# Attention and two gated layers on one core: the first batch's value products, one float32 product or split float32r products

## The chip, the cores and the metric

The kernel runs on one core of a Trainium2 chip. Its time is the device time of one execution in microseconds (us). The engines are PE (matrix products; PEld is its weight load), ACT (activations), DVE (vector), POOL and SP, which here only issues DMAs. Each engine takes its instructions in a fixed order and waits at one whose inputs are not there.

## The reference

Three steps follow each other: block-causal attention, a gated layer, and a gated layer behind a root-mean-square norm.

```
scores = scale * q @ k^T                 # 4 batches, 8 heads, 576 tokens, head width 64
mask   = row // 64 >= column // 64       # causal by blocks of 64 tokens
attn   = exp(scores - max) / (sum + 1e-9)
x      = attn @ v                        # then (2304, 512): all heads side by side
x      = ((x @ w_a) * (x @ w_b)) @ w_out # 512 -> 1536 -> 512
xn     = x / rms(x) * rms_g
out    = (silu(xn @ w_gate) * (xn @ w_val)) @ w_out2
```

Everything is float32 in and out.

## The kernel before

**Two ways to multiply.** A float32 product is one matmul in the program and two records of PE in the trace. A split product writes each operand as hi + lo, both of the type float32r (hi is a float32r copy, lo the remainder), and adds up the products of the parts; each of those is one record. The gated layers use split products throughout (`wh xh + wh xl + wl xh`, L598 to L600).

**Attention** goes by pairs of heads, 16 in all (4 batches, 4 pairs each); pair m has key tiles of 128 rows (index j) and 9 blocks of 64 queries (index b, L326: one buffer `pp8`, `pp7`, ... per b, shared by all pairs). A pair is done in two parts, blocks 0 to 5 and blocks 6 to 8. The generator `attention` (L306) lets three pairs' parts run abreast: in unit u it issues the value products of part u-2, the scores of part u, and the transposes of part u-1. For one part the chain is:

- `score` (L384): product of keys and queries on PE (L392, tiles `s` and `mm`), row maximum on DVE (L395, L398, L399), exponential on ACT with the row sum as a by-product (L401). After certain blocks DVE forms the reciprocals (L409, L410, tile `rt`) and POOL scales each block's probabilities with them (L413, tile `pp`).
- `p_transposes` (L416): PE transposes 128 x 128 squares, four to a PSUM bank (L428, tile `t`, three banks), and ACT copies a bank to SBUF (L431). For batches from WHOLE on the copy is hi (`ph`), and DVE writes lo (`pl`, L434) from the same bank. For batches below WHOLE the copy is plain float32 (`pw`), and there is no lo.
- The values. `whole_values` (L437), for batches below WHOLE: one float32 product per key tile for both heads at once (L453); of the result ACT copies one head and DVE the other to `xf` (L462, recorded at the copy helper's L109 and L111), in groups of four blocks at most. `values` (L469), for the others: per head one matmul with hi and one with lo of the probabilities (L488), against a tile `vv` that holds v's hi and lo side by side, so that both come out in one go in different partitions; ACT copies one half to `xf` (L493) and DVE adds the other (L494).
- `vv` is made by `make_vv` (L375) on POOL: a copy (L112) and a subtraction (L382). It is issued in unit u = 2m, two units ahead of its use; it returns at once where v was loaded whole.

v comes in by `load_v` (L353), two DMAs of SP per pair: below WHOLE with the heads interleaved in the tile (runs of 64 numbers), otherwise in runs of 5 x 64 numbers.

**Order of the work.** Batch 0's attention runs first (L885), with the first nine weight pieces made every ninth step of it (`prepare`, L189: loads by SP, decoding on ACT, DVE and POOL at L144 to L149, splitting at L109 and L119). Of the first gated layer only 27 matmuls can run beside it: three PSUM banks, three of the four column groups of x that are already there, three matmuls each. From there on the first gated layer's blocks run with batches 1 to 3 of attention between their matmuls, and the second gated layer at the end. Each engine's order is chosen by a scheduler that works out its own timeline when the program is built; so a changed instruction count moves neighbours too.

Of the kernel before, what the change touches and what calls it, by code (L numbers as in the profile page):

```python
# [25 lines left out]

BACKGROUND = (0, 4, 8, 24)

WHOLE = 1

RING = 19
UNSCALE = 2.0 ** -8
# [17 lines left out]
def tile_attention_moe_moe(  # L50
# [255 lines left out]
    def attention(pools, x_of, done):  # L306
# [46 lines left out]
        def load_v(m):  # L353
            b, h = divmod(m, H // 2)
            if b < WHOLE:
                t = vv[m] = ap2.tile([P, NTILE, 2, D], F32, tag="vr", name="vr", bufs=3)
# [59 lines left out]
        def p_transposes(u):  # L416
            m, part = divmod(u, 2)
            places = PLACE[part]
            whole = m // (H // 2) < WHOLE
            if whole:  # L420
# [90 lines left out]
        for u in range(2 * NP + 2):  # L511
            m, part = divmod(u, 2)
            if u >= 2:
                yield from (whole_values if (u - 2) // H < WHOLE else values)(u - 2)
            sc = list(SCORED[part]) if m < NP else []
# [592 lines left out]
```

## Time and profile before

| | |
|---|---|
| time, median of 3 runs | 1063.22 us (1061.3 to 1063.79) |
| the profiled execution's own time | 1065.04 us |
| its span in the trace | 1063.3 us |
| busiest engines, share of the span | PE 99%, DVE 63%, ACT 57%, POOL 37% |

Busy shares are averages over the whole span. The attention of batch 0 takes the first 77 us, and there PE is busy nine tenths of the time rather than all of it; the 80 us and more that follow show PE busy without a gap. A record of PE lasts longer than the time until the next record can begin, since matmuls overlap; so the cost of a run of matmuls is read from the start of the first to the start of what follows.

### The profile page before, as it was taken

Reading aid. Unit: us, or ns where it says so; the run is one execution under the profiler, and the core shown is the slowest. Engines: PE = TensorE matmul, PEld = TensorE weight load, DVE = VectorE, ACT = ScalarE, POOL = GpSimd, SP = SyncE. Lnnn points to the kernel's source line nnn. Section 1 sums busy time; section 2 is a strip of 40 time slices with the busy share of each in tenths; the row PEclk is TensorE's granted clock in tenths of the full one; section 3 lists DMA queues with packets and bytes.
Section 4 is the critical chain, followed back from the end, with each engine's and each line's share of the span. In section 5 each row is a group of like instructions: output and inputs, shape, how many; then the busy total and the mean of one; then the engine's idle time right before and its main releaser. Section 6 shows DMA issues by size and latency. Waiting matters only on the chain.

```text
span 1063.3 us, 16723 instructions
## 1 busy us (share of the span) xinstructions
PE 1048.8 (99%) x5644; PEld 933.9 (88%) x5644; DVE 669.4 (63%) x1299; ACT 602.1 (57%) x1334; POOL 396.5 (37%) x408
## 2 busy tenths in 40 slices
PE   9989999999999999999999999999999999999998
PEld 6668888889888888888878788999999999999998
DVE  6557778556675575385375724792876929657285
ACT  7878888557665664256444522744656546455352
POOL 5755668234444453175455501120231202212020
PEclk9999999999999999999999999999999999999999
DMA  9776877768986676878879763788889788887883
GB/s 240 223 237 217 283 243 279 283 226 275 310 309 209 218 250 239 315 260 315 343 277 358 271 257 134 225 281 255 251 280 326 259 273 250 290 270 229 275 249 116
DMA packets 121371, 276.52 MB, mean 260 GB/s; under 512 B 35779, under 2 KB 48835, under 8 KB 110790
## 3 DMA queue, kind: packets, MB, share of 16 engines
q1 hardware_dynamic: 121286, 275.46, 76.9%
q8 instruction: 45, 0.74, 0.3%
q14 instruction: 40, 0.33, 0.1%
HBM read 214.05 MB, written 61.36 MB: 259 GB/s over the span
## 4 chain that ended last, share of the span: by engine, by line
PE 77%; POOL 4%; issue 4%; DMA 4%; ACT 3%; DVE 2%; SPq 0%; POOLq 0%; ACTq 0%; DVEq 0%
PE mm L626 25%; PE mm L657 12%; PE mm L599 6%; PE mm L600 6%; PE mm L598 6%; PE s L392 5%; PE t L488 4%; PE t L428 3%; PE mm L558 3%; PE mm L560 3%; PE mm L559 3%; POOL src L149 2%; POOL bg L240 1%; DMA wc<-bg 1%; DMA st<-in_w_ab_dram 1%
## 5 line engine op out<-in xcount | busy, mean ns | idle before, releaser
L598 PE MATMUL mm<-xh,ab 128*128 128x512 f32 (+1 forms) x480 | 183.0, 384 | 0.0
L599 PE MATMUL mm<-xl,ab 128*128 128x512 f32 (+1 forms) x480 | 182.6, 380 | 0.0
L600 PE MATMUL mm<-xh,ab 128*128 128x512 f32 (+1 forms) x480 | 181.1, 377 | 0.0
L626 PE MATMUL mm<-hT,w 128*128 128x384 f32 x576 | 165.5, 337 | 1.4 <-ACT mm L634 1.4
L119 POOL TENSOR_TENSOR hl<-g,hh 128x384 fp32r<-128x384 f32 x36 | 42.7, 1187 | 299.6 <-ACT hh L109 299.6
L626 PE MATMUL mm<-hB,w 128*128 128x384 f32 x432 | 125.9, 336 | 0.0
L657 PE MATMUL mm<-hh,w 128*128 128x384 f32 x504 | 125.2, 336 | 0.0
L413 POOL TENSOR_SCALAR pp<-pp,rt 128x64 f32<-128x64 f32 (+3 forms) x144 | 79.9, 569 | 110.6 <-DVE rt L410 46.9
L634 ACT ACTIVATE mm<-mm 128x384 f32<-128x384 f32 x144 | 66.8, 474 | 75.3 <-PE mm L626 42.5
L626 PEld LDWEIGHTS mm<-hT,w 128*128 128x128 f32 x576 | 105.9, 188 | 2.8 <-ACT mm L634 2.5
L599 PEld LDWEIGHTS mm<-xl,ab 128*128 128x128 f32 x480 | 90.9, 189 | 16.7 <-issue 1.0
L600 PEld LDWEIGHTS mm<-xh,ab 128*128 128x128 f32 x480 | 90.9, 189 | 16.3 <-issue 0.7
L598 PEld LDWEIGHTS mm<-xh,ab 128*128 128x128 f32 x480 | 90.5, 189 | 16.3 <-issue 1.1
L626 PE MATMUL mm<-lT,w 128*128 128x384 f32 x288 | 96.9, 337 | 0.0
L392 PE MATMUL s<-ks,qz 128*128 128x64 f32 (+4 forms) x284 | 91.6, 412 | 2.4 <-ACT pp L401 2.3
L401 ACT ACTIVATE pp<-s,st 128x288 f32<-128x288 f32 (+8 forms) x142 | 70.2, 497 | 37.1 <-DVE st L395 28.9
L657 PEld LDWEIGHTS mm<-hh,w 128*128 128x128 f32 x504 | 90.6, 188 | 0.4 <-ACT mm L634 0.4
L657 PE MATMUL mm<-hl,w 128*128 128x384 f32 x252 | 81.4, 336 | 0.0
L626 PEld LDWEIGHTS mm<-hB,w 128*128 128x128 f32 x432 | 79.5, 188 | 0.0
L559 PE MATMUL mm<-hh,o 128*128 128x512 f32 (+1 forms) x208 | 79.3, 382 | 0.0
L558 PE MATMUL mm<-hh,o 128*128 128x512 f32 (+1 forms) x208 | 78.3, 377 | 0.5 <-DVE acc L568 0.5
L560 PE MATMUL mm<-hl,o 128*128 128x512 f32 (+1 forms) x208 | 76.6, 375 | 0.0
(146 smaller groups left out, 2317.4 us busy)
## 6 DMA issues: line engine op xcount, KB each, us to landing
w<-wc SPq DMA_DIRECT2D x252, 256.0 KB, 3.4
ab<-wab SPq DMA_DIRECT2D x36, 1024.0 KB, 5.6
w<-wco SPq DMA_DIRECT2D x126, 256.0 KB, 3.4
wc<-bg SPq DMA_DIRECT2D x12, 1792.0 KB, 6.8
o<-wo SPq DMA_DIRECT2D x12, 1536.0 KB, 7.4
st<-in_w_ab_dram SPq DMA_DIRECT2D x34, 512.0 KB, 4.8
wab<-ab SPq DMA_DIRECT2D x12, 1024.0 KB, 5.2
wco<-bg SPq DMA_DIRECT2D x6, 1792.0 KB, 7.0
```

The costliest lines, as they stand in the source:

```text
L392: pe.matmul(ps[:, 0:z - a], qz[m % 2][:, b], ks[m][:, a:z], start=True, stop=True)
L401: act.activation(pi[:, a:z], pss[x][:, 0:z - a], AF.Exp, bias=s[:, b:b + 1], scale=1.0, accum_out=t3[:, b, x:x + 1],)
L413: pool.tensor_scalar(t, t, r[:, y:y + 1], 1.0, ALU.mult, ALU.mult)
L558: pe.matmul(ps[:, 0:n], wh, hh, start=(y == 0), stop=False)
L559: pe.matmul(ps[:, 0:n], wl, hh, start=False, stop=False)
L560: pe.matmul(ps[:, 0:n], wh, hl, start=False, stop=(y == TF - 1))
L598: pe.matmul(ps[:, 0:n], wh[:, a:z], xhc, start=(c == 0), stop=False)
L599: pe.matmul(ps[:, 0:n], wh[:, a:z], xlc, start=False, stop=False)
L600: pe.matmul(ps[:, 0:n], wl[:, a:z], xhc, start=False, stop=(c == KC - 1))
L626: pe.matmul(ps, lhs, rhs[:, c, :], start=(start and c == 0 and y == 0), stop=(c == 1 and y == 2), skip_group_check=not start,)
L634: act.activation(to, ps, AF.Copy)
L657: pe.matmul(banks[m], lhs, rhs, start=(start and f == group[0] and y == 0), stop=(f == group[-1] and y == 2), skip_group_check=not start,)
```

## The change

```diff
-WHOLE = 1
+WHOLE = 0
```

With WHOLE at 0 no batch is below it. For the four pairs of batch 0, `load_v` takes the second form, `make_vv` does its two POOL operations, `p_transposes` writes `ph` and `pl` instead of `pw`, and `values` takes the place of `whole_values`. `whole_values` (L437 to L467) is not called any more. The code that batch 0 now goes through is that of batches 1 to 3:

```python
            copy(pool, hi, t)                                            # L381
            pool.tensor_tensor(lo, t, hi.bitcast(F32), ALU.subtract)
...
                    dve.tensor_tensor(lo, ps[:, 0:n], hi.bitcast(F32), ALU.subtract)   # L434
...
                act.activation(x[r, h, cols], ps[z, 0:n], AF.Copy)       # L493
                dve.tensor_tensor(x[r, h, cols], ps[r, 0:n], x[r, h, cols], ALU.add)
```

On POOL, at the first pair of heads, before (`pp_158` to `pp_163` are blocks b = 3 to 8, `rt` the reciprocals, `ks` the scaled keys of a later pair):

```order
L413 TENSOR_SCALAR pp_157<-pp_157,rt_139 128x192
L413 TENSOR_SCALAR pp_158<-pp_158,rt_139 128x256
L413 TENSOR_SCALAR pp_159<-pp_159,rt_139 128x320
L413 TENSOR_SCALAR pp_160<-pp_160,rt_139 128x384
L413 TENSOR_SCALAR pp_163<-pp_163,rt_139 128x576
L413 TENSOR_SCALAR pp_161<-pp_161,rt_139 128x448
L413 TENSOR_SCALAR pp_162<-pp_162,rt_139 128x512
L370 TENSOR_SCALAR ks<-kr 128x576
```

and now:

```order
L413 TENSOR_SCALAR pp_157<-pp_157,rt_139 128x192
L413 TENSOR_SCALAR pp_158<-pp_158,rt_139 128x256
L112 TENSOR_SCALAR vv<-vr 128x10x64
L413 TENSOR_SCALAR pp_159<-pp_159,rt_139 128x320
L413 TENSOR_SCALAR pp_160<-pp_160,rt_139 128x384
L112 TENSOR_SCALAR vv<-vr 128x10x64
L382 TENSOR_TENSOR vv<-vr,vv 128x10x64
L413 TENSOR_SCALAR pp_163<-pp_163,rt_139 128x576
L382 TENSOR_TENSOR vv<-vr,vv 128x10x64
L370 TENSOR_SCALAR ks<-kr 128x576
L413 TENSOR_SCALAR pp_161<-pp_161,rt_139 128x448
L413 TENSOR_SCALAR pp_162<-pp_162,rt_139 128x512
```

Two pairs' `vv` (a copy and a subtraction each) now stand between the normalisations of the first pair, and the part-1 blocks `pp_161` and `pp_162` come behind them and behind `ks`.

On DVE, where the second pair's scores and the first pair's transposes meet, before (`st` are row maxima, `x` a weight piece that is being decoded):

```order
L395 TENSOR_REDUCE st_138<-mm 128x1
L409 TENSOR_REDUCE rt_139<-su_141 128x2
L410 RECIPROCAL rt_139<-rt_139 128x2
L395 TENSOR_REDUCE st_138<-mm 128x1
L398 TENSOR_REDUCE st_138<-mm 128x1
L395 TENSOR_REDUCE st_138<-s 128x1 x2
L148 TENSOR_SCALAR x<-a 128x512
```

and now:

```order
L395 TENSOR_REDUCE st_138<-mm 128x1
L434 TENSOR_TENSOR pl_253<-t,ph_252 128x512
L395 TENSOR_REDUCE st_138<-mm 128x1
L409 TENSOR_REDUCE rt_139<-su_141 128x2
L398 TENSOR_REDUCE st_138<-mm 128x1
L410 RECIPROCAL rt_139<-rt_139 128x2
L148 TENSOR_SCALAR x<-a 128x512
L395 TENSOR_REDUCE st_138<-s 128x1
L434 TENSOR_TENSOR pl_253<-t,ph_252 128x512
L395 TENSOR_REDUCE st_138<-s 128x1
L434 TENSOR_TENSOR pl_253<-t,ph_252 128x512
L395 TENSOR_REDUCE st_138<-mm 128x1
```

Three subtractions `pl` have come in among the row maxima that release the exponentials. The second gated layer's order is the same in both.

## Rows read from the trace of the kernel before

**Rows 1.** The page's first part: busy time, share of the span, instructions.

```profile
PE 1048.8 (99%) x5644; PEld 933.9 (88%) x5644; DVE 669.4 (63%) x1299; ACT 602.1 (57%) x1334; POOL 396.5 (37%) x408
```

**Rows 2.** Stretches: us, busy us per engine (instructions), granted clock, DMA share, GB/s.

```profile
6.00:20.00 14.00, 13.98 (x65) 9.80 (x65) 10.94 (x34) 11.63 (x40) 7.51 (x13) 1.00 1.12 253
20.00:45.00 25.00, 21.85 (x107) 15.12 (x105) 14.18 (x43) 22.84 (x65) 18.57 (x25) 1.00 0.95 291
45.00:77.00 32.00, 28.54 (x138) 21.17 (x137) 17.06 (x42) 23.83 (x65) 20.42 (x25) 1.00 0.61 189
6.00:77.00 71.00, 64.37 (x305) 46.09 (x305) 42.18 (x117) 58.29 (x168) 46.50 (x62) 1.00 0.83 237
```

**Rows 3.** PE in time order: start, us, engine, line, operation [idle before].

```profile
17.80 1.03 PE L453 MATMUL t<-pw,vr 128*128 128x256 f32 x4
18.66 0.60 PE L428 MATMUL t<-ident,pp 128*128 128x128 f32 x4
```

**Rows 4.** PE in time order, split value products of batch 1.

```profile
105.54 0.27 PE L488 MATMUL t<-ph,vv 128*128 128x192 f32 x1
...
105.99 0.21 PE L488 MATMUL t<-ph,vv 128*128 128x64 f32 x1
...
106.15 0.55 PE L428 MATMUL t<-ident,pp 128*128 128x128 f32 x3
...
118.88 0.33 PE L488 MATMUL t<-pl,vv 128*128 128x384 f32 x1
119.06 0.28 PE L488 MATMUL t<-ph,vv 128*128 128x256 f32 x1
...
119.29 0.22 PE L488 MATMUL t<-ph,vv 128*128 128x128 f32 x1
119.35 0.38 PE L392 MATMUL s<-ks,qz 128*128 128x64 f32 x2
```

**Rows 5.** By line: instructions, ns min/median/max, first and last start, forms.

```profile
L434 DVE TENSOR_TENSOR pl<-t,ph x84: 278/682/694, 76.7 to 422.6; 128x512 fp32r<-128x512 f32 x72, 128x128 fp32r<-128x128 f32 x12
L494 DVE TENSOR_TENSOR xf<-t,xf x48: 329/449/562, 91.0 to 427.9; 64x384 f32<-64x384 f32 x24, 64x192 f32<-64x192 f32 x24
L493 ACT ACTIVATE xf<-t x48: 322/406/491, 90.5 to 427.0; 64x384 f32<-64x384 f32 x24, 64x192 f32<-64x192 f32 x24
L111 DVE COPY xf<-t x12: 294/360/428, 17.6 to 75.3; 64x256 f32<-64x256 f32 x4, 64x128 f32<-64x128 f32 x4, 64x192 f32<-64x192 f32 x4
L109 ACT ACTIVATE xf<-t x12: 253/314/400, 17.0 to 73.8; 64x256 f32<-64x256 f32 x4, 64x128 f32<-64x128 f32 x4, 64x192 f32<-64x192 f32 x4
L112 POOL TENSOR_SCALAR vv<-vr x12: 720/726/1167, 49.9 to 365.5; 128x640 fp32r<-128x640 f32 x12
L382 POOL TENSOR_TENSOR vv<-vr,vv x12: 1548/1568/2267, 52.9 to 366.4; 128x640 fp32r<-128x640 f32 x12
```

**Rows 6.** POOL in time order, pair 0's normalisation.

```profile
13.79 1.31 POOL L413 TENSOR_SCALAR pp<-pp,rt 128x448 f32<-128x448 f32 x2 [0.62 <-DVE rt L410]
```

**Rows 7.** DVE, POOL and ACT in time order around one stall.

```profile
20.43 0.69 DVE L119 TENSOR_TENSOR ab<-x,ab 128x512 fp32r<-128x512 f32 x1 [0.41 <-ACT ab L109]
...
52.87 2.11 DVE L119 TENSOR_TENSOR ab<-x,ab 128x512 fp32r<-128x512 f32 x1 [0.99 <-ACT ab L109]
55.01 0.43 DVE L148 TENSOR_SCALAR x<-a 128x512 uint32<-128x512 uint32 x1
...
52.88 1.55 POOL L382 TENSOR_TENSOR vv<-vr,vv 128x640 fp32r<-128x640 f32 x1
...
55.52 0.66 ACT L147 ACTIVATE a<-st 128x512 f32<-128x512 f32 x1 [2.69 <-issue]
...
75.59 0.60 ACT L431 ACTIVATE ph<-t 128x512 fp32r<-128x512 f32 x1 [1.52 <-PE t L428]
```

**Rows 8.** Stretches at the end of batch 0's attention, columns as in Rows 2.

```profile
76.00:80.00 4.00, 3.20 (x9) 2.39 (x10) 2.42 (x10) 2.86 (x9) 2.45 (x4) 0.71 1.06 437
80.00:84.00 4.00, 4.00 (x18) 2.68 (x18) 2.52 (x4) 2.55 (x7) 0.67 (x1) 0.86 0.12 47
```

## The prediction

> **What bounds the kernel now.** First the page's busy shares: PE works for 99% of the span [rows 1], so a change counts if it takes work from PE or lets PE stand idle. The product that goes is used in batch 0's attention alone, so I then cut out the stretch from 6 us (first scores) to 77 us (the first gated layer takes PE over) and read it in parts [rows 2]. The reader is to see three things there. PE is busy 64.4 of 71 us, so this stretch holds 6.6 us of PE idle, which is most of the kernel's 14.5 us (span 1063.3 less 1048.8 [rows 1]). Between 20 and 45 us ACT, not PE, is the fullest engine: 22.8 of 25 us against PE's 21.9. And in no part is one engine full while the others are free: over the 71 us ACT has 58.3, POOL 46.5, DVE 42.2. The stage is a ring: scores (PE), row maximum (DVE), exponential (ACT), scaling (POOL), transposes (PE), copies (ACT), and only then may the next pair's exponential overwrite the block. PE's saving is time only as far as the other three can follow.
>
> **PE: what goes and what comes.** A pair's whole products stream 512 + 4 x 256 columns in part 0 and 4 x 384 + 128 in part 1, 3200 in all. Two products of 256 columns take from 17.80 to 18.66 us, 0.86 us [rows 3], or 1.68 ns a column: 5.4 us a pair. The split products are 12 matmuls in part 0 (four each of 384, 256 and 128 columns) and 20 in part 1 (sixteen of 192, four of 64). Batch 1 shows their prices [rows 4]: 0.18 us for 384 columns (118.88 to 119.06), 0.115 for 256 (two to 119.29), 0.06 for 128 (to 119.35), 0.112 for 192 (four from 105.54 to 105.99) and 0.08 for 64 (two to 106.15). So 4 x 0.355 + 16 x 0.112 + 4 x 0.08 = 3.5 us a pair. PE is relieved of 1.85 us a pair, 7.4 us in four. This is the bound on the side of gain.
>
> **DVE: the largest addition.** Per pair seven subtractions `pl`, six at 0.68 and one at 0.28 us, make 4.4 us [rows 5]. The four additions to `xf` (two at 0.56, two at 0.33: 1.78 us) replace three copies at 0.36 (1.08): 0.7 us more. Together 5.1 us a pair, 20 us in four: DVE goes from 42.2 to 62.5 of 71 us.
>
> **ACT.** The copies of the transposes stay, hi instead of float32. To `xf` four copies (two at 0.49, two at 0.32: 1.62 us) replace three at 0.31 (0.94) [rows 5]: 0.7 us a pair, 2.7 us in four, 61.0 of 71.
>
> **POOL.** `vv` costs 0.73 + 1.57 us a pair [rows 5], 9.2 us in four: 55.7 of 71. The order puts two `vv` among pair 0's normalisations: 4.6 us ahead of `pp_161` and `pp_162`, which start at 13.79 us and end at 15.1 today [rows 6], so near 19.7 then. Queued behind are pair 0's last transposes, which PE reached only at 18.66 [rows 3]; with 1 us less of products ahead of them PE would be there at about 17.6 and wait a microsecond or two. Later `vv` fall where POOL has gaps.
>
> **At no cost.** v's DMAs come in longer runs, in the same number and place on SP. The second form of the values takes one step more per pair, so weight pieces are started one or two steps earlier; they use the same engines. Should a piece come later, the cover is the 27 early matmuls of the gated layer.
>
> **The sum.** By the end of the stage PE has 7.4 us less to do; the forecast is how much idle time takes its place. In the first 39 us (6 to 45) about 2.4 pairs pass DVE's new work and three `vv` pass POOL: DVE 25.1 + 12.2 = 37.3 us (96%), ACT 34.5 + 1.6 = 36.1 (93%), POOL 26.1 + 6.9 = 33 (85%), PE 35.8 - 4.4 = 31.4 (81%). The fullest engine there today reaches 92% (PE, 35.8 of 39). If DVE reaches the same 92%, the part needs 40.5 us, 1.5 more. One more DVE operation stretched as at 52.87 us (below) adds 1.4. In the last 32 us there is room (DVE 79%, ACT 78%, PE 80%), and waits of ACT for PE, such as the 1.52 us ahead of 75.59 [rows 7], can shrink: I take 1.5 us off. Sum 1.5 + 1.4 - 1.5 = +1.4 us on 1065.04, the profiled execution's own time. That execution lies 1.8 us above the median of the runs, 1063.22; against the median the sum is 1064.6, and I say 1065. PE's 7.4 us are then replaced by nearly 9 us of idle.
>
> **The unknown cost: DVE beside POOL.** At 52.87 us a DVE subtraction from SBUF took 2.11 us; the same form took 0.69 at 20.43. Beside the long one POOL ran a `vv` subtraction, from 52.88 for 1.55 us [rows 7]. Behind it DVE's `x` (55.01) came late, and ACT, which needed the buffer that `x` reads, stood 2.69 us until 55.52. The change brings four more such POOL subtractions. Below, the price is nothing (they meet `pl`, which reads only one operand from SBUF, the other from PSUM, and stays within 0.694 us in all its runs [rows 5]); above, 1.42 us each, 5.7 us. I take one of the four, since of the two `vv` that the stretch holds today one shows such a stall.
> The Trainium skill ("SBUF — State Buffer", Who interferes with whom) says that a DVE instruction with two inputs in SBUF contends with a GpSimd instruction that reads SBUF, and that the one that starts second is blocked for the whole of the other. The row at 52.87 us agrees: 0.69 + 1.55 is 2.24 against 2.11. By that rule alone every new `vv` is a possible block, which is the mechanism of the second rival.
>
> **Rivals.** *The relief arrives.* If the whole stage runs at 92% of its fullest engine, DVE with 62.5, it takes 67.9 us instead of 71: -3.1. If PE then enters the gated layer without a gap, the reduced clock there goes too: 0.71 of full speed from 76 to 80 us and 0.86 from 80 to 84 [rows 8], after a stretch in which PE was busy only 3.2 of 4 us, cost 1.2 + 0.6 = 1.7 us. Together -4.8: 1058.5; at the most the full 7.4, 1056. For it: ACT's 2.69 and 1.52 us of waiting were not ACT's own. Against it: 20 to 45 us, where ACT is at 91% already.
> *DVE and POOL hold each other up.* Place: the first 45 us, with three of the new `vv`. Price: 3 x 1.42 on DVE's 37.3 gives 41.6 us, at 92% 45.2, so +6.2, and the last part gives nothing back: 1069.5. It decides from the point where DVE's row maxima wait behind `pl` and stretched weight splits, so that exponentials start late and PE idles more than 17 us between 6 us and the takeover. For it: DVE at 96% without any stretch. Against it: `pl` itself is not stretched.
>
> **Chances.** Differences under 0.3% (3.2 us) can't be told from none. The forecast, 1061 to 1068, gets 0.42; relief 0.25; hold-up 0.33. Nearly all of the forecast's chance and 0.03 of either rival fall within 3.2 us of 1063.2; the forecast gives 0.05 to slower and 0.01 to faster. So faster 0.23, same 0.42, slower 0.35. The range, 1058 to 1071, cuts off only the ends of both rivals.
>
> **What would show it.** PE's idle time from 6 us to the first gated layer's uninterrupted run: near 15 to 16 us for the forecast (6.6 today), 10 to 11 for relief, above 20 for the hold-up. DVE's busy time over that stretch near 62 us; L488 in batch 0 at 3.5 us a pair; pair 0's `pp_161` on POOL near 18 us. After the stage PE should be busy without a gap as before; if the first gated layer then waits for weights, or if time is lost after 100 us, the reasoning is wrong, since all of it lies in the first 80 us.

## The result and the profile after

The changed kernel takes 1069.87 us (1069.22 to 1073.79) against 1062.95 (1061.3 to 1064.87) of the kernel before beside it: ratio 1.0072 [1.0055, 1.0089], slower. The forecast was 1065 with a range of 1058 to 1071, so the time lies in the range; the likeliest case, no measurable change, did not come. The price is nearly that of the hold-up rival (1069.5), but the experiments show that its mechanism is the smaller part of it. The profiled execution took 1070.42 us, its span is 1068.5.

First the page's busy shares and the stretches after, which answer to [rows 1] and [rows 2]; columns as there.

```profile
PE 1048.0 (98%) x5692; PEld 936.5 (88%) x5692; DVE 692.9 (65%) x1331; ACT 606.2 (57%) x1338; POOL 406.3 (38%) x416
```

```profile
6.00:20.00 14.00, 11.45 (x51) 7.27 (x50) 10.28 (x30) 10.69 (x38) 9.41 (x14) 1.00 0.98 264
20.00:45.00 25.00, 20.23 (x101) 15.06 (x100) 19.75 (x49) 19.51 (x51) 19.52 (x26) 0.86 0.75 235
```

The reader is to see three things. No engine has become full: DVE, which the forecast saw at 96% up to 45 us, has 10.28 + 19.75 = 30.0 of 39 us there (77%), ACT 30.2, POOL 28.9, and PE fell from 35.8 to 31.7. The loss begins at once: PE is busy 11.5 of the first 14 us against 13.98. And the granted clock is 0.86 of full speed from 20 to 45 us, where it was 1.00.

Busy time hides part of the loss, for a record of PE lasts longer when nothing follows it closely or when the clock is low. Starts are safer. The table gives the start of each pair's first transpose (L428), of the 28th matmul of the first gated layer (the takeover, since 27 run early), and the time lost by 100 us. Lost time is 100 us less the issue time of all matmuls that started until then, each counted at the spacing that it has in a run without gaps (those of the prediction for the value products, but 0.05 us for 64 columns; 0.11 us a transpose; for the others 0.84 ns a column in a float32 record and 0.42 in a float32r one, with some ns on top). Lost times without a decimal are good to about half a microsecond. Each row is one execution: that of before took 2.1 us more than the median of its kernel, that of e1 1.5 less, that of e3 3.1 more.

| kernel | pair 0 | pair 1 | pair 2 | pair 3 | pair 4 | takeover | lost by 100 us |
|---|---|---|---|---|---|---|---|
| before | 10.5 | 27.0 | 42.9 | 60.2 | 74.3 | 77.2 | 15.6 |
| after | 11.0 | 32.1 | 50.7 | 66.3 | 82.7 | 87.4 | 29.2 |
| e1 | 10.9 | 31.6 | 47.7 | 63.3 | 79.7 | 84.4 | 26.2 |
| e2 | 11.2 | 30.6 | 46.3 | 60.4 | 74.8 | 80.7 | 22.8 |
| e3 | 11.1 | 33.9 | 50.3 | 67.1 | 83.5 | 88.2 | 30 |
| e4 | 10.5 | 26.2 | 41.8 | 56.6 | 72.4 | 74.6 | 15.7 |
| e5 | 10.7 | 28.1 | 44.9 | 60.3 | 75.9 | 78.4 | 22 |
| e6 | 10.8 | 27.2 | 42.0 | 57.6 | 73.4 | 79.4 | 23.0 |
| e7 | 11.3 | 29.0 | 48.4 | 63.0 | 78.8 | 80.5 | 24 |
| e8 | 10.7 | 26.2 | 40.2 | 56.5 | 74.0 | 78.7 | 20.8 |
| e9 | 10.5 | 25.4 | 39.9 | 55.1 | 70.7 | 73.5 | 15.8 |
| e10 | 11.2 | 27.7 | 42.2 | 57.8 | 73.6 | 79.6 | 23.2 |
| e11 | 10.6 | 26.5 | 42.2 | 56.8 | 73.3 | 75.3 | 17 |
| e12 | 11.5 | 25.4 | 40.2 | 55.2 | 69.7 | 74.6 | 17.3 |

In the whole kernel PE's issue time went from 1036.0 to 1028.0 us: the relief is there, 8 us of it. The lost time by 100 us grew by 13.6. Together +5.6 us, and the span grew by 5.2 (the median by 6.9); after 100 us both kernels lose nearly the same (span less issue time less the loss by 100 us: 11.7 and 11.3 us). So all of it lies in batch 0's attention, most of it in the first two turns of the ring: from pair 0 to pair 1 21.1 us instead of 16.5, from pair 1 to pair 2 18.6 instead of 15.9.

**The first turn.** ACT in time order, before, in the middle of pair 0 (start, us, engine, line, operation):

```profile
13.40 0.61 ACT L431 ACTIVATE pw<-t 128x512 f32<-128x512 f32 x1
...
14.33 0.63 ACT L431 ACTIVATE pw<-t 128x512 f32<-128x512 f32 x1
14.87 0.68 ACT L144 ACTIVATE ld<-ld 128x512 uint32<-128x512 uint32 x1
```

and after:

```profile
15.42 0.67 ACT L144 ACTIVATE ld<-ld 128x512 uint32<-128x512 uint32 x1 [1.64 <-DMA ld<-in_w_ab_dram]
15.98 0.65 ACT L147 ACTIVATE a<-ld 128x512 f32<-128x512 f32 x1
16.54 0.29 ACT L401 ACTIVATE pp<-s,st 128x64 f32<-128x64 f32 x1
...
16.83 0.58 ACT L431 ACTIVATE ph<-t 128x512 fp32r<-128x512 f32 x1
...
17.76 0.60 ACT L431 ACTIVATE ph<-t 128x512 fp32r<-128x512 f32 x1
```

Before, pair 0's second and third copy of transposes (L431) stand ahead of the first weight decoding (L144, L147). After, the decoding stands ahead of them, and its weights are not there yet: ACT stands still for 1.64 us, decodes for another 1.1, and the two copies start at 16.83 and 17.76 instead of 13.40 and 14.33, 3.4 us late. PE sees it through an exponential (16.54) that is queued behind the decoding too. PE after, the gaps up to pair 0's last value products:

```profile
16.98 0.81 PE L392 MATMUL s<-ks,qz 128*128 128x320 f32 x2 [1.60 <-ACT pp L401]
...
22.54 1.47 PE L428 MATMUL t<-ident,pp 128*128 128x128 f32 x12
24.89 0.33 PE L428 MATMUL t<-ident,pp 128*128 128x128 f32 x1 [0.87 <-DVE pl L434]
26.33 0.43 PE L392 MATMUL s<-ks,qz 128*128 128x64 f32 x2 [1.12 <-ACT pp L401]
```

PE waits 1.60 us until 16.98 and reaches pair 0's last transposes at 22.54, not at 18.66 [rows 3]. Behind them it runs dry, for DVE and for ACT; the `pl` that it needs at 27.47 stood on DVE behind the weight split that runs from 25.21 for 1.60 us (row further down). And then its clock goes. Stretches of after:

```profile
24.00:28.00 4.00, 1.31 (x9) 0.97 (x8) 3.48 (x6) 4.00 (x13) 2.26 (x3) 1.00 1.04 298
28.00:30.00 2.00, 2.00 (x12) 1.89 (x11) 1.82 (x8) 2.00 (x6) 0.00 (x0) 0.68 1.00 275
30.00:34.00 4.00, 4.00 (x18) 3.34 (x17) 0.91 (x1) 1.71 (x6) 3.53 (x5) 0.50 0.56 141
34.00:36.00 2.00, 2.00 (x6) 1.21 (x6) 1.91 (x5) 1.54 (x6) 2.00 (x3) 0.61 0.58 228
```

From 24 to 28 us PE is busy 1.31 of 4 us, while ACT has no pause (4.00 of 4). Behind that the granted clock is 0.68, 0.50 (the 1.2 GHz level) and 0.61: PE works all 8 us and gets 0.64 + 2.0 + 0.78 = 3.4 us less done. Before had no such stretch until 76 us [rows 8].

**The second turn.** SP's issues before:

```profile
18.79 0.38 SPq L340 DMA_DIRECT2D kr<-in_k_dram  x1
```

and after:

```profile
18.93 2.77 SPq L362 DMA_DIRECT2D vr<-in_v_dram  x4
21.80 0.38 SPq L340 DMA_DIRECT2D kr<-in_k_dram  x1
```

Before, SP issues pair 3's k at 18.79. After, four DMAs of v stand ahead of it, those of two pairs: `make_vv` copies v away early, the buffer is free sooner, and the load that waited for it moves up in SP's order. k is issued at 21.80. What waits for it on POOL, before:

```profile
28.49 0.67 POOL L370 TENSOR_SCALAR ks<-kr 128x576 f32<-128x576 f32 x1 [1.50 <-DMA kr<-in_k_dram]
```

and after:

```profile
30.47 0.68 POOL L370 TENSOR_SCALAR ks<-kr 128x576 f32<-128x576 f32 x1 [4.21 <-DMA kr<-in_k_dram]
31.11 1.28 POOL L149 TENSOR_TENSOR x<-x,ld 128x512 uint32<-128x512 uint32 x1
```

Then ACT after:

```profile
32.43 0.63 ACT L109 ACTIVATE ab<-x 128x512 fp32r<-128x512 f32 x1 [2.21 <-POOL x L149]
```

And DVE after (two of its rows are spoken of further down):

```profile
25.21 1.60 DVE L119 TENSOR_TENSOR ab<-x,ab 128x512 fp32r<-128x512 f32 x1 [0.38 <-ACT ab L109]
...
27.34 0.41 DVE L148 TENSOR_SCALAR x<-a 128x512 uint32<-128x512 uint32 x1
...
33.09 1.13 DVE L119 TENSOR_TENSOR ab<-x,ab 128x512 fp32r<-128x512 f32 x1 [3.12 <-ACT ab L109]
...
35.50 1.55 DVE L148 TENSOR_SCALAR x<-a 128x512 uint32<-128x512 uint32 x1
```

POOL stands 4.21 us in front of `ks`, which waits for that k and starts at 30.47 instead of 28.49; behind `ks` is a weight piece (L149), for it ACT waits 2.21 us with `ab`, and for that DVE 3.12 us (33.09). One late load stops three engines in a row.

### The profile page after: what moved, and what is told of

It reads as the page before. It is cut to its first block, busy times and chain, and to the rows that moved or that the text cites. A ratio compares the mean times of both kernels' runs of the same rounds, so it can differ in the third digit from the quotient of the medians.

```text
span 1068.5 us, 16878 instructions
## 1 busy us (share of the span) xinstructions
PE 1048.0 (98%) x5692; PEld 936.5 (88%) x5692; DVE 692.9 (65%) x1331; ACT 606.2 (57%) x1338; POOL 406.3 (38%) x416
## 4 chain that ended last, share of the span: by engine, by line
PE 89%; DMA 4%; ACT 3%; DVE 3%; issue 1%; POOL 0%; SPq 0%; POOLq 0%; ACTq 0%; DVEq 0%
PE mm L626 25%; PE mm L657 12%; PE mm L599 9%; PE mm L598 9%; PE mm L600 9%; PE s L392 5%; PE t L488 4%; PE mm L558 4%; PE mm L560 4%; PE mm L559 4%; PE t L428 3%; DMA xf<-x_dram 1%; DMA qz<-in_q_dram 1%; ACT pp L401 1%; DMA kr<-in_k_dram 1%
## 5 line engine op out<-in xcount | busy, mean ns | idle before, releaser
L119 POOL TENSOR_TENSOR hl<-g,hh 128x384 fp32r<-128x384 f32 x36 | 42.8, 1188 | 299.5 <-ACT hh L109 299.5
L413 POOL TENSOR_SCALAR pp<-pp,rt 128x64 f32<-128x64 f32 (+3 forms) x144 | 80.5, 574 | 107.9 <-DVE rt L410 59.8
L599 PEld LDWEIGHTS mm<-xl,ab 128*128 128x128 f32 x480 | 90.5, 189 | 15.8 <-issue 0.7
L434 DVE TENSOR_TENSOR pl<-t,ph 128x512 fp32r<-128x512 f32 (+1 forms) x112 | 68.7, 627 | 28.3 <-ACT ph L431 27.5
L558 PE MATMUL mm<-hh,o 128*128 128x512 f32 (+1 forms) x208 | 79.6, 383 | 1.9 <-ACT acc L566 0.9
```

The lines of the kernel that those rows point to most:

```text
L413: pool.tensor_scalar(t, t, r[:, y:y + 1], 1.0, ALU.mult, ALU.mult)
L434: dve.tensor_tensor(lo, ps[:, 0:n], hi.bitcast(F32), ALU.subtract)
L558: pe.matmul(ps[:, 0:n], wh, hh, start=(y == 0), stop=False)
L599: pe.matmul(ps[:, 0:n], wh[:, a:z], xlc, start=False, stop=False)
```

## The experiments

All times are ratios to the kernel before on the same chip; e1 to e4 ran on one chip, e5 to e8 on a second, e9 to e12 on a third, so that a ratio from one of these groups is compared with one from another only by way of before. Five theories are named in the expectations: **K**, k late behind v on SP; **W**, weight decoding ahead of pair 0's copies on ACT; **V**, the operations of `vv` between pair 0's normalisations on POOL; **D**, DVE too full with `pl` and held up by POOL (the prediction's hold-up); **P**, the load of `vv` on POOL, and its holding up of DVE. F and E stand in e5's expectation alone. `behind(instruction, "name")` keeps an instruction after the one last stored in `gate["name"]`; it adds an order, no wait. In the kernel, `gate["act"]` is already the last copy of transposes.

**e1: k first.**

```diff
-                sp.dma_start(out=t, in_=k[b, h])
+                gate["k"] = sp.dma_start(out=t, in_=k[b, h])
...
-                sp.dma_start(out=t[:, hh], in_=v[b, 2 * h + hh])
+                behind(sp.dma_start(out=t[:, hh], in_=v[b, 2 * h + hh]), "k")
```

> The changed kernel with one order restored on SP: a pair's two v loads may not be issued ahead of that pair's k load. Theory K (the k load of pair 3 is queued behind 640 KB of v that the change lets SP issue earlier; POOL stands 4.2 us at it, and ACT, DVE and PE behind): k is issued about 3 us earlier, POOL's wait at 30.5 us shrinks below 2 us, the half clock from 28 to 36 us goes, the time falls from +7 us over before to +2 to +4. Theory D (the lo subtractions on DVE among the row maxima hold the exponentials up): at most 1 us is gained, +6 to +7 us stay. Theory P (the vv work on POOL): no change either.

1.0046 [1.0032, 1.0060], down from 1.0072. Pair 3's k is now issued at 18.29, as SP shows:

```profile
18.29 0.33 SPq L340 DMA_DIRECT2D kr<-in_k_dram  x1
```

and on POOL its `ks` starts at 25.24:

```profile
25.24 0.67 POOL L370 TENSOR_SCALAR ks<-kr 128x576 f32<-128x576 f32 x1 [0.47 <-DMA kr<-in_k_dram]
```

The second turn is 16.1 us instead of 18.6, near before's 15.9; the first is still 20.7. The half clock, which theory K expected to go, stays; it comes earlier:

```profile
24.00:32.00 8.00, 6.71 (x30) 6.35 (x31) 5.29 (x13) 5.52 (x16) 5.35 (x7) 0.57 1.07 281
```

The time is 4.4 us above before, just outside the 2 to 4 that theory K had. K is a part of the loss, and not the larger; the slow clock came with the long first turn, and goes with it in e6.

**e2: k first, no `pl` in batch 0** (with e1's edit; the kernel leaves out the lo part of the probabilities, its second product reads `ph`).

```diff
-                if not whole:
+                if m < H // 2:
+                    pass
+                elif not whole:
                     lo = ...
```

> As e1, and for batch 0 DVE's subtractions pl are left out: the second matmul of each pair of value products reads ph in place of pl, so PE's work is the same (that part of the computation is left out). 28 subtractions, 17.5 us of DVE, are gone. Theory D: PE's lost time in the first 100 us falls back to that of before (15.6 us) or below, while PE's 8 us of saved work stay: 4 to 8 us faster than before. Theory K: what e1 leaves stays, within 1.5 us of e1. Theory P: the same as K.

1.0039 [1.0027, 1.0052] against e1's 1.0046. All 28 subtractions, some 17 us of DVE's work, are gone, and in the time almost nothing is gained. But that is not the price of `pl`: by 100 us this kernel has lost 3.4 us less than e1 (table), though ACT's wait in front of the first decoding is longer, 2.56 us. It loses the gain again far behind batch 0's attention, e1 first, then e2:

```profile
130.00:150.00 20.00, 20.00 (x103) 16.18 (x101) 15.92 (x33) 15.54 (x34) 14.86 (x16) 1.00 0.63 235
130.00:150.00 20.00, 16.86 (x81) 12.22 (x80) 15.60 (x31) 14.70 (x35) 13.01 (x15) 1.00 0.60 213
```

PE stands idle there for 3.1 us (the longest wait, 1.68 us, is for a split on DVE), and 22 records of matmuls fewer fall in. Ahead of that wait a weight split on DVE took 2.06 us (142.04) beside a `vv` subtraction of batch 1 on POOL (142.00, 1.55 us), the stretch that the prediction had read at 52.87. The edit displaced other work too; what of it empties PE at this place was not tried. So e2's ratio doesn't decide on D.

**e3: k first, no subtraction for v's lo in batch 0** (with e1's edit).

```diff
-            pool.tensor_tensor(lo, t, hi.bitcast(F32), ALU.subtract)
+            if m < H // 2:
+                pool.memset(lo.bitcast(F32), 0.0)
+            else:
+                pool.tensor_tensor(lo, t, hi.bitcast(F32), ALU.subtract)
```

> As e1, and for batch 0 POOL writes zeros in place of v's lo part (that part is left out): four subtractions of 1.57 us that read SBUF become four writes that read nothing. Theory P (POOL's load and its holding up of DVE): 2 to 4 us below e1, and DVE's longest weight splits (1.6 us and 1.1 us between 20 and 37 us) fall to 0.7. Theory D and K: within 1 us of e1.

1.0033 [1.0022, 1.0045]. Against e1 0.0013 less, with intervals that overlap: no clear price for POOL's four long subtractions, and so for their meeting with DVE. DVE's weight splits between 20 and 40 us did fall to 0.75 and 0.68 us, as theory P had it, but L148 still took 1.54 us at 25.68.

**e4: split products for pairs 2 and 3 alone.**

```diff
-            if b < WHOLE:
+            if m in (0, 1):
```

(and the same condition where `p_transposes` and the choice of `values` ask for the batch)

> Half of the change: pairs 0 and 1 of batch 0 keep the one float32 product, pairs 2 and 3 have split products. Half of PE's saving, 4 us, remains. Theory D with its place in the first 45 us, and theory K: the first 45 us look as before, there is room after that, and the kernel is 0 to 3 us faster than before. If the price is the same for each pair: half of +7, so 3 to 4 us slower.

0.9978 [0.9968, 0.9989]: faster than before. Half of the change gains 0.2% of the time, near 2.3 us where PE is relieved of 3.7. So the split products with their `pl` need not make the kernel slower; it depends on which pairs take them. In this kernel ACT's copies of pair 0 stand where they stood before.

**e5: pairs 1, 2 and 3** (condition `m in (0,)`, with e1's edit).

> Pair 0 keeps the one float32 product, pairs 1 to 3 are split, and k goes first on SP as in e1. Theory F (the price is paid in the first turn of the ring, between pair 0's and pair 1's transposes, where e1 still takes 20.7 us and before 16.5): the first turn is back near 16.5 us, and the kernel is 2 to 4 us faster than before, a little better than e4 (pairs 2 and 3). Theory E (every early pair costs, pair 1 as much as pair 0): half of e1's +4.4 us stays, so +1 to +2 us.

1.0056 [1.0037, 1.0075]: with pair 0 as before the loss is still there. But it is no longer where theory F has it. The first turn is 17.4 us, near the 16.5 that F expected, the second 16.8, and the clock is full up to the takeover; yet by 100 us some 22 us are lost, spread over the whole attention. What holds this kernel is not shown. ACT in it, around pair 0's copies:

```profile
13.74 0.63 ACT L431 ACTIVATE pw<-t 128x512 f32<-128x512 f32 x1
...
15.56 0.71 ACT L144 ACTIVATE ld<-ld 128x512 uint32<-128x512 uint32 x1 [0.74 <-DMA ld<-in_w_ab_dram]
...
16.71 0.61 ACT L431 ACTIVATE pw<-t 128x512 f32<-128x512 f32 x1
```

The decoding (L144) again stands ahead of a copy of pair 0, the third, with 0.74 us of waiting for its weights. Theory W, formed from the same order in e1 and the changed kernel, explains at most a small part here, since the first turn is only 0.9 us longer than in before.

**e6: k first, weights decoded later** (with e1's edit). The second of the decoding's two ACT steps is kept behind the last copy of transposes too (the first is so already), and the first two preparation steps (8 and 17) become one (14), behind all three copies of pair 0's first part; every later piece then comes nine steps later:

```diff
-        act.activation(a, hi.bitcast(F32), AF.Prelu, scale=2.0 ** -111, alpha=-(2.0 ** 32))
+        behind(act.activation(a, hi.bitcast(F32), AF.Prelu, scale=2.0 ** -111, alpha=-(2.0 ** 32)), "act")
...
-        if n % 9 == 8 and prepared[0] < 2 * TF + TF:
+        if n % 9 == (8 if n > 20 else 5) and n > 8 and prepared[0] < 2 * TF + TF:
```

> As e1 (all four pairs split, k first), and ACT's first two decoding steps of a weight piece are kept behind pair 0's three transposed copies, where they stand in the kernel before; in e1 and in the changed kernel they stand two copies earlier, and ACT waits 1.6 us there for the weights' DMA. Theory W (that wait starts the slack that empties PE and lets its clock fall): PE's wait for ACT near 17 us goes, and 2 to 4 us of e1's +4.4 go. Theory V (the two vv on POOL ahead of pair 0's part-1 scaling): under 1 us.

0.9997 [0.9988, 1.0007], from e1's 1.0046 on another chip. ACT:

```profile
12.30 0.59 ACT L431 ACTIVATE ph<-t 128x512 fp32r<-128x512 f32 x1
...
14.50 0.60 ACT L431 ACTIVATE ph<-t 128x512 fp32r<-128x512 f32 x1 [0.70 <-PE t L428]
...
15.44 0.60 ACT L431 ACTIVATE ph<-t 128x512 fp32r<-128x512 f32 x1
17.01 0.68 ACT L144 ACTIVATE ld<-ld 128x512 uint32<-128x512 uint32 x1 [0.98 <-DMA ld<-in_w_ab_dram]
```

All three copies shown, those of pair 0's first part, now come first, and the wait for the weights falls behind them. The first turn is 16.4 us (before 16.5, e1 20.7), and PE's clock stays at 1.00 up to 77 us. This edit is worth the most of any. The edit has two halves, the order on ACT and the later step, and they were not run apart. Together they do more than theory W says: they also thin out the decoding, since up to 45 us ACT starts four operations of L147 here, six in e1 and in the changed kernel, and seven in before. How much of the gain is the order at pair 0's copies, and how much the lighter load behind, is not shown.

**e7: k first, `vv` later** (with e1's edit): `make_vv`'s copy is kept behind the pair's scaling on POOL.

```diff
-                        pool.tensor_scalar(t, t, r[:, y:y + 1], 1.0, ALU.mult, ALU.mult)
+                        gate["norm"] = pool.tensor_scalar(t, t, r[:, y:y + 1], 1.0, ALU.mult, ALU.mult)
...
-            copy(pool, hi, t)
+            behind(copy(pool, hi, t), "norm")
```

> As e1, and POOL's vv of pair 1 is kept behind all the scaling of pair 0, which then ends about 2.3 us earlier. Theory V: pair 0's part-1 transposes come 2 us earlier, the first turn shortens from 20.7 to about 18.5 us, and 2 us of e1's +4.4 go. Theory W: under 1 us, since PE is held by ACT's wait ahead of that.

1.0033 [1.0019, 1.0046]; against e1 the intervals overlap. The first turn did shorten, to 17.7 us, but the second grew from 16.1 to 19.4. Little of V's price shows in the time while W is there.

**e8: all three** (the edits of e1, e6 and e7).

> The edits of e1, e6 and e7 together. If W and V are separate waits in one chain, their gains add: the first turn near 16.5 us, the clock keeps its level, and the kernel with all four pairs split is within 1 us of before or up to 3 us faster. If the ring is bound elsewhere (ACT at over nine tenths between 20 and 45 us), it stays 2 us or more slower than before.

0.9972 [0.9962, 0.9983], faster than before by 3 us, with no instruction of the change taken away. Against e6 V is now worth 0.25%, with intervals apart. Its stretches:

```profile
6.00:20.00 14.00, 13.30 (x66) 9.13 (x64) 11.12 (x36) 11.55 (x39) 10.96 (x16) 1.00 1.00 282
20.00:45.00 25.00, 22.88 (x135) 16.92 (x134) 22.06 (x58) 24.31 (x69) 21.29 (x29) 1.00 0.85 263
```

PE is busy 13.3 and 22.9 us here (after 11.5 and 20.2) and the clock is 1.00. That DVE and ACT are fuller than in the changed kernel (22.1 and 24.3 of 25 us) fits a ring that turns faster.

**e9: the kernel before with the later decoding alone** (e6's second edit on the kernel before): a control.

> The kernel before with the later weight decoding of e6 and nothing else (nothing is left out of the computation). Control for W. If W is a repair of what the change displaced (the first decodings had slid ahead of pair 0's copies on ACT), the kernel before, whose decodings already stand behind those copies, gains nothing: ratio 0.998 to 1.002. If the edit is a gain of its own for any kernel (decoding at a better place), it speeds up before as it sped up the changed kernel: ratio 0.994 to 0.997.

1.0026 [1.0013, 1.0040]: slower, which neither theory had. Up to the takeover this kernel is quicker than before (pair 4 at 70.7 instead of 74.3), and gives it back there. Its stretches around the takeover, and then those of before:

```profile
70.00:80.00 10.00, 6.35 (x18) 3.42 (x17) 6.88 (x14) 4.20 (x12) 8.06 (x11) 0.81 0.69 256
```

```profile
70.00:80.00 10.00, 8.29 (x29) 5.42 (x28) 5.62 (x17) 6.90 (x20) 5.65 (x9) 0.88 0.58 226
```

PE is busy 6.35 of 10 us against 8.29, and the clock is lower. (The two executions shown take nearly the same time, spans of 1062.9 and 1063.3; the 0.26% is in the medians.) So the later decoding is not a gain for any kernel; but it isn't a mere repair either, since the attention gained by it. The trace shows what PE stands at: 2.64 us until 77.10 for an exponential, which waits for a row maximum, which stands on DVE behind a weight split (L119) that runs from 74.58 for 1.78 us, while POOL makes a split too (74.55, 1.26 us). In before this weight split took 0.88. Whether it is the cause of the 0.26% wasn't tried.

**e10: the changed kernel with the later decoding alone** (e6's second edit, v free to go ahead of k).

> The changed kernel with the later weight decoding alone; v's loads are again free to be issued ahead of the pair's k load (nothing is left out of the computation). W (decodings ahead of pair 0's copies on ACT) took 1.0046 to 0.9997 when k was already first. If the order of v and k on SP (K) and W are separate prices, this run keeps K's 0.26% on top of e6: ratio 1.002 to 1.004. If the late k load only hurts because PE was already late from W, K vanishes here: ratio 0.9985 to 1.001.

1.0011 [0.9997, 1.0025], between the two theories, and its interval overlaps e6's. SP issues k later than in e6, at 18.48 instead of 15.71, and yet POOL has `ks` at the same time in both, first e6, then e10:

```profile
26.55 0.84 POOL L370 TENSOR_SCALAR ks<-kr 128x576 f32<-128x576 f32 x1 [3.33 <-DMA kr<-in_k_dram]
```

```profile
26.64 0.67 POOL L370 TENSOR_SCALAR ks<-kr 128x576 f32<-128x576 f32 x1 [3.00 <-DMA kr<-in_k_dram]
```

All starts in the table differ by 0.5 us at most from e6's. So the order on SP is worth little here; but not because a late k no longer hurts, for POOL stands 3 us for k in both. Issuing it earlier no longer brings it earlier. From 1.0072 this edit alone takes back 0.6%, e1's alone 0.26%.

**e11: pairs 2 and 3 split, all three edits.**

> Split value products for batch 0's pairs 2 and 3 only (pairs 0 and 1 as before), with all three repairs: k ahead of v on SP, decoding later on ACT, values' copies behind the normalisation on POOL (nothing is left out of the computation). e4 had these two pairs without the repairs at 0.9978 and lost no time beyond before's. If the repairs mend only what pairs 0 and 1 displaced, they have nothing to mend here: ratio 0.997 to 0.999. If they are worth their 0.5% in any kernel, 0.993 to 0.995.

0.9971 [0.9958, 0.9983], against e4's 0.9978: the edits mend what pairs 0 and 1 displaced and are worth little where nothing was. It is as fast as e8 with half of the change: the splits of pairs 0 and 1 bring nothing more there.

**e12: e8 without `pl` in batch 0** (e8's edits and e2's).

> e8 (all three repairs, all four pairs split) without the 28 subtractions pl of batch 0: its lo product reads hi instead, so the lo part of the probabilities is left out there and 17 us of DVE work are gone. If DVE is what keeps the rest of PE's saving from becoming time once the orders are repaired (the prediction's sum: the fullest engine sets the pace), this run gains most of what is still missing: ratio 0.992 to 0.994 against e8's 0.9972. If the rest is lost elsewhere (ACT's order, POOL, the gated layer's start), it stays near e8: 0.996 to 0.998.

0.9944 [0.9929, 0.9958]. Here the same 28 subtractions cost 0.28%, 3 us, and the lost time by 100 us falls from 20.8 to 17.3 (before 15.6). That is 3.5 us, as in e2 (3.4); but here nothing is lost behind it, PE is busy for all of 130 to 150 us. So D is real in both kernels, and e2's ratio hid it. The ratio lies between the two expectations: 4 to 5 us of PE's 7.4 had failed to become time in e8, and `pl` accounts for 3.

## Why the prediction was right and wrong

**PE: right.** L488 in batch 0 has the prices read from batch 1. PE after, two pairs' value products:

```profile
54.67 0.55 PE L488 MATMUL t<-ph,vv 128*128 128x384 f32 x1
...
56.15 0.34 PE L488 MATMUL t<-ph,vv 128*128 128x384 f32 x1
56.33 0.34 PE L488 MATMUL t<-pl,vv 128*128 128x384 f32 x1
...
63.46 0.27 PE L488 MATMUL t<-ph,vv 128*128 128x192 f32 x1
...
64.12 0.39 PE L488 MATMUL t<-ph,vv 128*128 128x64 f32 x2
```

384 columns take 0.18 us from start to start (56.15 to 56.33), and six products of 192 stand from 63.46 to 64.12, 0.11 us each: 3.5 us a pair as forecast, and 8.0 us less issue time in the whole kernel (7.4 forecast; the difference is the price taken for 64 columns). The first row is a lone 384: 0.55 us of busy time for the same work. That is why the test that the prediction set, PE's idle time up to the takeover, misled. Up to 87.4 us:

```profile
6.00:87.40 81.40, 68.99 (x366) 51.13 (x364) 61.70 (x157) 65.89 (x182) 56.74 (x72) 0.96 0.69 215
```

PE is idle 12.4 us there, which by the prediction's scale lies between relief and forecast, though the takeover came 10.2 us late. Idle time is not lost time where records stretch.

**DVE's and POOL's additions: right in size.** By line and form, after, 6 to 88 us (count, then busy us and mean ns, then the idle before them):

```profile
L434 DVE TENSOR_TENSOR pl<-t,ph 128x512 fp32r<-128x512 f32 x27 | 18.4, 685 | 1.6 <-ACT ph L431 1.2
...
L382 POOL TENSOR_TENSOR vv<-vr,vv 128x640 fp32r<-128x640 f32 x6 | 9.6, 1595 | 0.3
...
L148 DVE TENSOR_SCALAR x<-a 128x512 uint32<-128x512 uint32 x11 | 7.4, 672 | 1.7 <-ACT a L147 1.6
```

`pl` costs 0.685 us, as in [rows 5], and the subtraction of `vv` 1.6. ACT's copies to `xf` (L493) have means of 0.485 and 0.325 us, as forecast.

**DVE beside POOL: right in kind, too dear.** The forecast took one more stretch of 1.4 us. At 25.21 us a subtraction from SBUF took 1.60 us, at 35.50 L148 took 1.55 where 0.41 is usual (27.34). POOL beside them:

```profile
24.98 1.28 POOL L149 TENSOR_TENSOR x<-x,ld 128x512 uint32<-128x512 uint32 x1
35.50 1.26 POOL L119 TENSOR_TENSOR ab<-x,ab 128x512 fp32r<-128x512 f32 x1
```

Both started beside a weight piece and not beside a new `vv`; in before an L148 of 1.11 us (18.91) stands beside an L149 too. Beside the new `vv` the longest was an L148 of 1.17 us, at 16.67. The eleven L148 and the seven subtractions at L119 up to the takeover add up, row by row, to 13.15 us before and 13.56 after, +0.4 us. The Trainium skill ("SBUF — State Buffer", Who interferes with whom) has both kinds: two inputs from SBUF contend with a GpSimd instruction that reads SBUF, and a tensor_scalar in a two-port mode contends with GpSimd; an instruction with one SBUF input outside these modes does not. The traces agree, since `pl` isn't stretched. By its rule each new `vv` could have blocked DVE; e3, without the four, is 0.0013 lower in its ratio than e1, within overlapping intervals.

**POOL at pair 0: right in place, late by more.** `pp_161` was forecast at 18 us and started at 19.67, behind 1.47 us of waiting of `ks` for its k. PE reached the last transposes at 22.54, not at 17.6 and a microsecond or two, behind ACT's late copies; in e6, with the copies first, the first turn is 16.4 us.

**"At no cost": the step that failed.** "v's DMAs come in longer runs, in the same number and place on SP": they were not in the same place; four of them passed pair 3's k. "Weight pieces are started one or two steps earlier; they use the same engines": what cost time is not the step. The first piece is started at step 8 in both programs, before any value product; and still the scheduler put its decoding ahead of two of pair 0's copies, in the queue of an engine that the ring needs, and in front of weights that had not landed. The prediction looked for the price of coming late (the 27 early matmuls) and not for that of standing ahead of others. e10 and e1 price these at 0.6% and 0.26%, each alone (lost time by 100 us: 6.0 and 3.0 of the 13.6 us); some of the first is more than repair, since e9's attention gained by the edit too and e6's edit also thins out the decoding. The prediction read the orders of POOL and DVE; ACT's, which was to be had just as well, held the largest effect, and SP's another.

**The sum.** It had +2.9 us for the first 39 us and -1.5 for the last 32. Pair 2's first transposes came at 50.7 instead of 42.9, +7.8, and from there to pair 4's it was 32.0 us against 31.4. The rule behind it, a fullest engine at 92%, didn't apply: over these 39 us DVE and ACT reached 77% and PE 81%, and the ring stood in waits. In e8, where the orders are mended, the ring does reach that level, but with other engines: PE has 36.2 of 39 us (93%), ACT 35.9 (92%), DVE 33.2 (85%). That `pl` costs 3 us there, with DVE not the fullest engine, is not what the rule supposes; it fits a chain in which work waits for `pl`, as PE does at 27.47.

**The rivals.** The hold-up's 1069.5 was met by luck. Of its cause `pl` is worth 3.4 us of the 13.6 lost (e2 against e1), and its other part, DVE stretched beside the new `vv`, shows no clear price (e3); most of the rest is in the two orders (6.0 and 3.0, each alone), which it did not have. That the time lies within the stated range is luck as well: the range reached up to 1071 for this rival's sake. The relief's price, 4.8 us below before, was too good for the change with its orders mended: e8 gains 3.

## What to carry to other kernels

When a change alters what a program-order scheduler sees, compare the order on every engine and DMA queue, above all on those to which the change adds nothing; an instruction that moved ahead of its data stops everything behind it. A piece of work that moves up in a queue isn't free: ask what stands behind it if its input isn't there. And when you take an operation away to price it, read the traces by stages before you believe the ratio: the removal moves other work, and can lose elsewhere what it gained (e2 gained 3.4 us in the attention and lost them behind it, so that 0.07% was left; e12 kept them, 0.28%).

## What was not expected of the hardware

After PE had been busy 1.31 us of 4, its clock was at or near the 1.2 GHz level for some 8 us, although it was busy throughout; so the gap cost more than twice its length here (2.7 us of idle, and 3.4 of slow clock behind it). And a DMA that is issued later need not land as much later: pair 3's k, issued 3.0 us later (21.80 against 18.79), let POOL start 2.0 us later (30.47 against 28.49); in e10, issued 2.8 us later than in e6, it let POOL start at the same time (26.64 against 26.55).
